# A retention and two-layer mixture kernel on one Trainium2 core: its opening written in the program's own order, with the loads laid out anew

## The chip, the cores and the metric

One NeuronCore of a Trainium2 chip runs the whole program. The metric is device time in microseconds (us), lower is better. The core has five engines with a queue of their own: PE (TensorE, the matrix engine), DVE (VectorE), ACT (ScalarE), POOL (GpSimd) and SP (SyncE, which here only issues DMAs). Each engine takes its instructions strictly in the order in which they stand in its queue.

## What is computed

Attention with a decay instead of a softmax, over 4 batches, 8 heads, 576 positions and 64 channels, feeds a mixture of 4 experts (all used for each token, weighted by given probabilities), which feeds a second mixture of 8 experts of which each token uses one.

```python
scores = scale * np.matmul(q, k.transpose(0, 1, 3, 2))
Dmat = np.where(rel >= 0, gamma[:, None, None] ** rel[None, :, :], 0.0)
x = np.matmul(scores * Dmat[None], v)            # -> 2304 tokens x 512
for e in range(4):                               # first mixture, hidden width 1024
    h = np.maximum(x @ w1[e], 0.0)
    out += p[:, e:e + 1] * (h @ w2[e])
...                                              # second mixture: one of 8 experts per token
```

## The kernel before, in words

Attention goes in 36 steps of 64 positions (`NSTEP`, 9 steps to a batch). Step s has four small groups of float32 matmuls, 8 instructions each (the trace counts 16, two passes to an instruction): the scores (`at_scores`, L258, tile `sc<-qkr`), what the state of the past adds (`at_past`, L278, `uo<-qkr,sn`), scores times values (`at_b`, L290, `uo<-pf,vkr`), and the step's share of the next state (`at_state`, L302, `uo<-vkr,ks`). Between them stand DVE's masking of the scores (`pf`, L268), its four updates of the state (`sn`, L327; `at_sum`) and its scaling of the result (`xf`, L344), POOL's decayed keys (`ks`, L242; `at_split`), and the split of the result into two float16 parts: the high part on ACT (L346), the low part on DVE for the first block, on POOL later (`at_out`, L348 and L350).

Every large product is made of three float16 products of such halves. So the weights are split too: `w_load` brings a float32 piece of 512 KB into one of four buffers `wr`, `w_split` makes the high half on ACT (L191) and the low half on DVE (L192), twice for each piece. Tokens go in 9 blocks of 256 (`NB`), which is four steps to a block. The first expert's first layer (`l1_first`, L533, `ph<-xc,wm`) has four units of 48 matmuls for a block; for block 0 each unit comes in halves of 24 matmuls of 128 columns, so that steps 0 and 1 are enough for the first halves. After a unit, ACT and DVE make the two halves of the hidden values (`keep`, `ht`, L519 and L520). The second layer (`l2`, L685, `po<-wm,ht`) has four units of 12 matmuls of 512 columns for a block. While it runs, `at_hook` adds an attention step after each unit, and `w_do` takes from a list (`w_todo`) the loads and mixings that make sums of the weight quarters for later experts (`mix`, L461 and L462; `x_mix`, `x_keep` and `x_store`, L357, L365, L366 and L369, do the same for x).

What sets the order: in the kernel before, the opening (L1088 to L1157) is written in Python in a certain order, and the tile framework's scheduler then puts the instructions of each engine in an order of its own; where the text says `tc.issue_after`, an instruction may not stand ahead of a given one. SP takes a load only when its buffer is free, and in its queue's order, so a load that waits holds up all behind it. The opening writes a few loads, then runs `opening(s)` for steps 0 to 5, each with the split of step s + 2 and the loads of step s + 4 behind it, with weight splits and half units between them. In `at_step(s)` the scores and the state of step s + 1 go ahead of the result of step s.

Of the kernel before, what the change touches and what calls it, by code (L numbers as in the profile page):

```python
# [126 lines left out]
    return at, np.ascontiguousarray(np.concatenate(cols, axis=1))  # L127


@with_exitstack  # L130
def kernel(
    ctx: ExitStack,
# [88 lines left out]
    def at_load(s):  # L221
        load_qk(s)
        load_vk(s)
# [75 lines left out]
            if uos[s][2] is not None:  # L299
                after(mm, uos[s][2])  # L300

    def at_state(s, on):  # L302

        if s % NC == NC - 1:
            return
        t, ks = raws[s]
        uo = uos[on][0]
        for h in HEADS:
            b2, b1, b0 = _bits(h)
            pe.matmul(  # L310
                uo[rows(b0 ^ b1), b0, C * b2:C * b2 + C], lhsT=ks[rows(b1), 2 * b2 + b0],
                rhs=t[rows(b1), 8 + b2 if b0 else 2 * b2 + b1], start=first(on, b0, b0 ^ b1), stop=True, skip_group_check=True,
            )

    def at_sum(s, on):
        c = s % NC
        if c == NC - 1:
            return
        u = uos[on][0][:, :, 0:2 * C].rearrange("p a (b d) -> p a b d", b=2)
        sn = at_1.tile([128, 2, 2, D], F32, name="sn")  # L320
        if c == 0:
            dve.tensor_copy(out=sn, in_=u)
        else:
            old = st[s - 1]
            for i in range(4):
# [44 lines left out]

    def at_step(s):

        at_open(s)
# [7 lines left out]
        at_out(s)  # L381

    def ago(s, b):
        return s - max(NS * b + NS - 1, NS + 1)
# [39 lines left out]
            sp.dma_start(out=r, in_=w1[e, :, i])  # L424
        rw[e, i] = r

    def w_split(e, i):
        r = rw.pop((e, i))
        if i < KD:
            r = r.rearrange("p (k f) -> p k f", k=KD)  # L430
            for k in range(2):
                t = w1_part(k, i // 2)[:, :, :, 256 * (i % 2):256 * (i % 2) + 256]
                split(r[:, 2 * k:2 * k + 2], t[:, :, 0], t[:, :, 1], S_W)
        else:
            j = 2 * (i - KD)
            for k in range(2):
                split(
                    r[:, 512 * k:512 * k + 512].rearrange("p (h d) -> p h d", h=2), w2_row(j + k, 0), w2_row(j + k, 1), S_W
                )

# [237 lines left out]
    def l2(b, i, h):  # L678
        t = b * TB + i
        if h == 0:  # L680
            pos[b, i] = ps_o[0].tile([128, 2, DM // 2], F32, tag="o", name="po")
        po = pos[b, i]
        for k in range(4 * h, 4 * h + 4):
            for n, (x, y) in enumerate(TERMS):
                pe.matmul(  # L685
                    po,
                    lhsT=hts[k // 2][:, x, k % 2, i * 128:(i + 1) * 128],
                    rhs=w2_row(k, y),
                    start=(k == 0 and n == 0),
                    stop=(k == KF - 1 and n == 2),  # L690
                )
        if h:
            act.activation(out=acc[:, t, 0:DM].rearrange("p (a d) -> p a d", a=2), in_=po, func=ACTF.Copy, scale=p_sb[:, t, 0:1])
# [391 lines left out]
        )  # L1085


    at_load(0)  # L1088
    sp.dma_start(out=ka, in_=ca)
    at_load(1)  # L1090
    w_tiles(0)
    w_load(0, 0, True)
    at_load(2)
    w_load(0, 1, True)
    w_load(0, 2, True)
    at_load(3)
    w_load(0, 3, True)
    dve.memset(acc[:, :, DM:ROW], 0.0)
    pool.memset(acc[:, BM * TB:, 0:DM], 0.0)
# [9 lines left out]
    at_split(0)  # L1109
    at_scores(0)  # L1110
    at_open(-1)
    at_state(0, -1)
    at_sum(0, -1)
    at_split(1)
    opening(0)
    opening(1)
    w_split(0, 0)
    w_load(0, 4)
    l1_first(0, 0, 0, 1)
    w_split(0, 1)  # L1120
    w_load(0, 5)
    l1_first(0, 1, 0, 1)
    opening(2)
    w_split(0, 2)
    w_load(0, 6)
    l1_first(0, 2, 0, 1)
    w_split(0, 3)
    w_load(0, 7)
    sp.dma_start(out=p_sb, in_=probs)
    opening(3)  # L1130
    l1_first(0, 3, 0, 1)
    l1_first(0, 0, 1, 2)
    w_split(0, 4)
    opening(4)
    l1_first(0, 1, 1, 2)
    w_split(0, 5)
    l1_first(0, 2, 1, 2)
    w_split(0, 6)
    opening(5)
    l1_first(0, 3, 1, 2)  # L1140
    w_split(0, 7)
# [4 lines left out]
    sp.dma_start(out=wgr, in_=wg)  # L1146
    sp.dma_start(out=kb, in_=cb)
    sp.dma_start(out=k16, in_=c16)
    ps_sum = at_1.tile([128, NT, 1], F32, name="ps_sum", bufs=1)
    dve.tensor_reduce(out=ps_sum, in_=p_sb, axis=AX.X, op=ALU.add)  # L1150
    dve.tensor_scalar(out=ps_sum, in0=ps_sum, scalar1=1e-9, scalar2=None, op0=ALU.add)
    ps_inv = at_1.tile([128, NT, 1], F32, name="ps_inv", bufs=1)
    dve.reciprocal(out=ps_inv, in_=ps_sum)
    dve.scalar_tensor_tensor(
        out=p_sb, in0=p_sb, scalar=SO1, in1=ps_inv.to_broadcast([128, NT, E1]), op0=ALU.mult, op1=ALU.mult
    )
    split(wgr, wg_sb[:, 0], wg_sb[:, 1], S_G)  # L1157

    nxt = [NS + 2]
    n_stage = 16 * E2  # L1160
# [5 lines left out]
    def at_hook():  # L1166
        s = nxt[0]
        if s >= NSTEP + 4:
            return
        nxt[0] += 1  # L1170
        if s + 4 < NSTEP:
            load_vk(s + 4)
        if s + 3 < NSTEP:
            load_qk(s + 3)
        if s + 2 < NSTEP:
            at_split(s + 2)
        for b in range(NB):
            if ago(s, b) == 1:
                x_mix(b, 0)
        if s < NSTEP:  # L1180
            at_step(s)
        for b in range(NB):
            n = ago(s, b)
            if n == 2:
                x_store(b, 0)
# [280 lines left out]
```

## Time and profile before

| | us |
|---|---|
| runs shown: lowest, median, highest of 3 | 996.5, 999.72, 1002.97 |
| the profiled execution's own time | 998.96 |
| span of its instructions | 997.0 |
| PE busy in the span | 960.9 |

The span is the time from the first to the last instruction of the profiled execution; its own time is 1.96 us longer. In the timeline a row gives the start (us from the span's start), the duration, engine, source line, operation, the tile written and those read, how many instructions are put together, and in brackets how long the engine had been idle before and what released it. "PEclk" is the clock that TensorE was granted as a share of its full 2.4 GHz; 0.5 is 1.2 GHz.

### The profile page before, as it was taken

The page shows a single profiled execution, that of the slowest core. Times are in us where ns is not written, and L with a number is a line of the kernel's source. Part 1 is how long each engine was busy: PE and PEld are TensorE (multiplying, and loading weights), DVE is VectorE, ACT ScalarE, POOL GpSimd, SP SyncE. Part 2 cuts the span into 40 slices and gives each one's busy share as a digit, 9 for nine tenths or more (in the row PEclk, how much of TensorE's full clock was granted, in tenths as well). Part 3 has the DMA queues.
Part 4 walks back from the last instruction along what each step waited for, and adds up shares of the span by engine and source line. Part 5 has one row for each costly group of instructions (what it writes and reads, how often), then busy time and mean ns, then how long its engine had stood idle before and what let it go on. Part 6 is the DMA issues. An engine that isn't in the chain of part 4 may idle for free. (4 is left out here: it accounts for less than half of the span.)

```text
span 997.0 us, 31905 instructions
## 1 busy us (share of the span) xinstructions
PE 960.9 (96%) x13507; PEld 827.5 (83%) x13507; DVE 577.3 (58%) x1296; ACT 534.2 (54%) x1017; POOL 411.7 (41%) x433
## 2 busy tenths in 40 slices
PE   5799999999999999999999999999999999999995
PEld 5576667899999999999999999999987677777773
DVE  5765571475677777766776775888888211211210
ACT  3445453677767777776787686676643122212221
POOL 3577764645555244455442454342323222112111
PEclk9999999999999999999999999999999999999998
DMA  9879774345457778467668726879835616554691
GB/s 335 283 260 328 279 236 166 109 126 181 165 185 217 231 257 270 133 207 211 207 195 309 251 80 174 251 208 232 234 113 199 233 44 229 207 218 146 256 393 48
DMA packets 95939, 209.48 MB, mean 210 GB/s; under 512 B 21486, under 2 KB 42222, under 8 KB 93488
## 3 DMA queue, kind: packets, MB, share of 16 engines
q1 hardware_dynamic: 82784, 159.20, 48.0%
q0 software_dynamic: 13008, 48.20, 15.2%
q8 instruction: 108, 1.77, 0.7%
q14 instruction: 39, 0.32, 0.1%
HBM read 197.88 MB, written 52.99 MB: 252 GB/s over the span
## 5 line engine op out<-in xcount | busy, mean ns | idle before, releaser
L646 PEld LDWEIGHTS <-op 128*128 128x128 f16 x2604 | 245.6, 98 | 26.0 <-POOL s L197 0.7
L580 POOL TENSOR_TENSOR op<-sm,op 128x512 f16<-128x512 f32 x124 | 142.2, 1157 | 223.9 <-ACT op L579 223.8
L561 PEld LDWEIGHTS <-wm_a 128*128 128x128 f16 x3264 | 192.9, 98 | 3.9
L561 PE MATMUL ph<-xc,wm_a 128*128 128x128 f16 x2112 | 132.2, 219 | 0.0
L579 ACT ACTIVATE op<-sm 128x512 f16<-128x512 f32 x124 | 77.6, 634 | 86.7 <-DVE sm L584 86.7
L1068 DVE SCALAR_TENSOR_TENSOR h_s<-p_h,h_s 128x512 f16<-128x512 f32 x40 | 27.6, 691 | 159.1 <-ACT h_s L1067 144.1
L1075 PE MATMUL p_y<-wm_a,h_s 128*128 128x512 f16 x480 | 107.2, 379 | 0.5 <-DVE h_s L1068 0.5
L646 PE MATMUL pv<-wm_a,op 128*128 128x256 f16 x792 | 97.4, 273 | 0.0
L646 PE MATMUL px<-wm_a,op 128*128 128x256 f16 x744 | 91.3, 272 | 0.7 <-DVE acc L654 0.7
L1075 PEld LDWEIGHTS <-h_s 128*128 128x128 f16 x480 | 46.7, 98 | 52.4 <-DVE h_s L1068 0.7
L207 DVE TENSOR_TENSOR s<-pz,s 128x512 f16<-128x512 f32 x111 | 74.0, 683 | 15.6 <-ACT s L206 15.6
L561 PEld LDWEIGHTS <-wm_b 128*128 128x128 f16 x1296 | 76.9, 98 | 1.4
L1078 POOL DMA_INDIRECT out_dram<-y_s,sidxm x17 | 17.2, 1013 | 146.4 <-ACT y_s L1077 128.9
L205 ACT ACTIVATE pz<-sr 128x512 f32<-128x512 f32 x111 | 65.6, 605 | 14.4 <-DVE rk L804 8.8
L464 POOL TENSOR_TENSOR wr<-wr 128x512 f32<-128x512 f32 x48 | 60.4, 1270 | 29.9 <-ACT pz L205 29.2
L1067 ACT ACTIVATE h_s<-p_h 128x512 f16<-128x512 f32 x40 | 23.9, 597 | 78.9 <-PE p_h L1058 74.9
L206 ACT ACTIVATE s<-pz 128x512 f16<-128x512 f32 x111 | 64.0, 599 | 0.6
L1077 ACT ACTIVATE y_s<-p_y,x_g 128x512 f32<-128x512 f32 x20 | 13.7, 687 | 92.8 <-PE p_y L1075 79.2
L654 DVE SCALAR_TENSOR_TENSOR acc<-px,p_sb,acc 128x256 f32<-128x256 f32 x124 | 59.2, 478 | 7.3 <-PE px L646 7.0
L1058 PEld LDWEIGHTS <-wm_b 128*128 128x128 f16 x1056 | 60.0, 98 | 2.8 <-issue 0.6
L1058 PE MATMUL p_h<-x_s,wm_b 128*128 128x128 f16 x1056 | 61.5, 219 | 0.3 <-issue 0.2
L205 ACT ACTIVATE pz<-wr 128x512 f32<-128x512 f32 x100 | 59.4, 609 | 1.5 <-DVE wm_a L207 1.1
(208 smaller groups left out, 1787.3 us busy)
## 6 DMA issues: line engine op xcount, KB each, us to landing
wm_a<-w2d SPq DMA_DIRECT2D x20, 2048.0 KB, 9.6
wr<-in_w_dram SPq DMA_DIRECT2D x40, 512.0 KB, 7.1
wm_b<-w1d SPq DMA_DIRECT2D x10, 2048.0 KB
wm_a<-w1d SPq DMA_DIRECT2D x10, 2048.0 KB
sr<-in_w1s_dram SPq DMA_DIRECT2D x64, 256.0 KB, 3.8
w1d<-s SPq DMA_DIRECT2D x64, 256.0 KB, 4.7
sr<-in_w2s_dram SPq DMA_DIRECT2D x64, 256.0 KB, 5.1
w2d<-s SPq DMA_DIRECT2D x64, 256.0 KB, 4.7
```

Source lines behind the costliest of these rows:

```text
L205: act.activation(out=z, in_=raw, func=ACTF.Copy, scale=scale)
L206: act.activation(out=hi, in_=z, func=ACTF.Copy)
L207: dve.tensor_tensor(out=lo, in0=z, in1=hi, op=ALU.subtract)
L464: pace["pool"] = pool.tensor_tensor(out=quarter(e, n, k, to), in0=quarter(e, n, k, x), in1=quarter(e, n, k, y), op=op)
L561: pe.matmul(bank[:, i], lhsT=w[:, k, u, 128 * i:128 * i + 128], rhs=x[:, v, d, k], start=(first and i == 0 and n == 0), stop=(n == 5), ski ...
L579: act.activation(out=hi, in_=s, func=ACTF.Copy)
L580: pool.tensor_tensor(out=lo, in0=s, in1=hi, op=ALU.subtract)
L646: pe.matmul(out, lhsT=o[a][:, v, k], rhs=w[c][:, k, u], start=(first and n == 0), stop=(n == 11), skip_group_check=True,)
L654: step = dve.scalar_tensor_tensor(out=a, in0=src, scalar=p_sb[:, b * TB + i, e:e + 1], in1=a, op0=ALU.mult, op1=ALU.add)
L1058: pe.matmul(ph[:, j], lhsT=w[k][:, x, f * 128:(f + 1) * 128], rhs=xs[:, y, k], start=(n == 0), stop=(n == 3 * KD - 1),)
L1068: dve.scalar_tensor_tensor(out=lo, in0=ph, scalar=0.0, in1=hi, op0=ALU.max, op1=ALU.subtract)
L1075: pe.matmul(po, lhsT=h[:, a, k], rhs=w[k][:, b], start=(n == 0), stop=(n == 3 * KF - 1))
```

## The change

The opening is rewritten, and each of its instructions is tied to the order in which the program text has it.

- A wrapper `InOrder` around the five engines calls `tc.keep_in_program_order` on every instruction until the opening's end, so the scheduler no longer moves them. In a profile of the changed kernel all of these instructions carry the wrapper's line, L139.
- The loads all stand ahead of the opening, in a new order: the constants `ka` ahead of the first values, the fourth piece of w1 directly behind the second and third, then alternately the pieces of w2 and the steps 4 to 9.
- `at_out` is taken apart into `at_x` (DVE) and `at_parts` (ACT and POOL), and the low half of x is made on POOL for block 0 as well.
- The state of step s stands right ahead of step s (`opened`), no longer in step s - 1. The low half of the second part of two of the four pieces of w2 is made on POOL (`split_p`).
- The seventh step's (s = 6) decayed keys, scores and state, which stood in the opening, now stand in the first unit of layer 2, behind the opening's last POOL instruction; x's mixing and storing on POOL may not stand ahead of the POOL instruction before it; the list of weight mixings begins two units later.

```diff
+class InOrder:
+    def __getattr__(self, name):
+        f = getattr(self.engine, name)
+        def issue(*args, **kw):
+            return self.tc.keep_in_program_order(f(*args, **kw))
+        return issue
...
-    pe, act, dve, pool, sp = nc.tensor, nc.scalar, nc.vector, nc.gpsimd, nc.sync
+    pe, act, dve, pool, sp = [InOrder(tc, e) for e in (nc.tensor, nc.scalar, nc.vector, nc.gpsimd, nc.sync)]
...
         act.activation(out=hi, in_=xf, func=ACTF.Copy)
-        if b:
-            pace["pool"] = pool.tensor_tensor(out=lo, in0=xf, in1=hi, op=ALU.subtract)
-        else:
-            dve.tensor_tensor(out=lo, in0=xf, in1=hi, op=ALU.subtract)
+        pace["pool"] = pool.tensor_tensor(out=lo, in0=xf, in1=hi, op=ALU.subtract)
...
+    for i in range(1, KD):
+        w_load(0, i, True)
+    at_load(3)
+    w_load(0, KD)
+    at_load(NS)
+    w_load(0, KD + 1)
+    at_load(NS + 1)
+    w_load(0, KD + 2)
+    w_load(0, KD + 3)
...
     def opening(s):
-        at_step(s)
-        at_split(s + 2)
-        load_vk(s + 4)
-        if s < NS + 1:
-            load_qk(s + 4)
+        at_open(s)
+        at_past(s)
+        at_b(s)
+        at_x(s)
+
+    def opened(s):
+        at_state(s, s - 1)
+        at_sum(s, s - 1)
+        del uos[s - 1]
...
+    l1_first(0, 0, 1, 2)
+    w_split(0, KD)
+    l1_first(0, 1, 1, 2)
+    later_step(NS)
+    at_split(NS + 1)
+    w_split(0, KD + 1, split_p)
+    l1_first(0, 2, 1, 2)
+    later_step(NS + 1)
+    l1_first(0, 3, 1, 2)
+    w_split(0, KD + 2)
+    w_split(0, KD + 3, split_p)
...
+        if s == NS + 2:
+            with tc.issue_after(pace["pe"].ins), tc.issue_after(pace["pool"].ins):
+                at_split(s)
+                at_split(s + 1)
+                at_split(s + 2)
+                at_open(s)
+                at_scores(s)
+                at_state(s, s, 4 * C)
+                at_sum(s, s, 4 * C)
...
-            if (b, u) == (0, 0):
+            if (b, u) == (0, 2):
                 w_todo.extend([w_loads(0, 0, 2), w_loads(0, 1, 3)] + w1_steps(0) + [lambda: None])
```

The order of PE's first instructions before: the scores of the first three steps stand ahead of the first state.

```order
L263 MATMUL sc<-qkr 64x64 x24
L310 MATMUL uo<-vkr,ks 64x64 x8
L295 MATMUL uo<-pf,vkr 64x64 x8
L310 MATMUL uo<-vkr,ks 64x64 x8
L286 MATMUL uo<-qkr,sn 64x64 x8
L295 MATMUL uo<-pf,vkr 64x64 x8
L310 MATMUL uo<-vkr,ks 64x64 x8
L263 MATMUL sc<-qkr 64x64 x5
```

And now, up to the third step's last group, behind which the first unit of layer 1 stands.

```order
L139 MATMUL sc<-qkr 64x64 x8
L139 MATMUL uo<-vkr,ks 64x64 x8
L139 MATMUL sc<-qkr 64x64 x8
L139 MATMUL uo<-pf,vkr 64x64 x8
L139 MATMUL uo<-vkr,ks 64x64 x8
L139 MATMUL uo<-qkr,sn 64x64 x8
L139 MATMUL uo<-pf,vkr 64x64 x8
L139 MATMUL sc<-qkr 64x64 x8
L139 MATMUL uo<-vkr,ks 64x64 x8
L139 MATMUL uo<-qkr,sn 64x64 x8
L139 MATMUL uo<-pf,vkr 64x64 x8
```

The groups of steps 0 and 1 moved ahead of the third step's scores; the fourth step's scores, which stood here, moved behind three half units.

SP's queue before, from the first piece of w1 to the first two pieces of w2 (`qkr` and `vkr` are a step's queries with keys, and its values with keys; `wr` with 4x256 is a piece of w1, with 1024 one of w2).

```order
L422 DMA wr<-in_w_dram 128x4x256
L228 DMA qkr<-in_qk_dram 128x640
L234 DMA vkr<-in_vk_dram 128x640
L422 DMA wr<-in_w_dram 128x4x256 x2
L228 DMA qkr<-in_qk_dram 128x640
L234 DMA vkr<-in_vk_dram 128x640
L422 DMA wr<-in_w_dram 128x4x256
L234 DMA vkr<-in_vk_dram 128x640
L228 DMA qkr<-in_qk_dram 128x640
L234 DMA vkr<-in_vk_dram 128x640
L228 DMA qkr<-in_qk_dram 128x640
L420 DMA wr<-in_w_dram 128x1024 x2
```

And the same stretch now.

```order
L139 DMA wr<-in_w_dram 128x4x256
L139 DMA qkr<-in_qk_dram 128x640
L139 DMA vkr<-in_vk_dram 128x640
L139 DMA wr<-in_w_dram 128x4x256 x3
L139 DMA qkr<-in_qk_dram 128x640
L139 DMA vkr<-in_vk_dram 128x640
L1196 DMA wgr<-in_wg_dram 128x64
L1197 DMA kb<-in_cb_dram 128x330
L1198 DMA k_84<-in_c_dram 128x256
L139 DMA wr<-in_w_dram 128x1024
L139 DMA qkr<-in_qk_dram 128x640
L139 DMA vkr<-in_vk_dram 128x640
```

The fourth piece of w1 moved ahead of the fourth step's two loads, three small tables that were loaded much later moved into the opening, and the pieces of w2 stand one by one between the steps.

POOL's queue now, from the keys of step 5 (`ks_570`) to those of steps 6, 7, 9 and 10 (`ks_720`, `ks_722`, `ks_811`, `ks_851`; step 8 needs none). `wm` are low halves of w2, `xc_565` the low half of block 1's x, `xf_207` block 0's x, whose sums are made in place.

```order
L139 TENSOR_TENSOR ks_570<-vkr_139,ka_101 128x256
L139 TENSOR_TENSOR wm_c_82<-wr_135,wm_c_82 128x2x256
L139 TENSOR_TENSOR xc_565<-xf_566,xc_565 128x4x64
L139 TENSOR_TENSOR wm_a_78<-wr_143,wm_a_78 128x2x256
L256 TENSOR_TENSOR ks_720<-vkr_147,ka_101 128x256
L256 TENSOR_TENSOR ks_722<-vkr_152,ka_101 128x256
L373 TENSOR_TENSOR xf_207<-xf_207 128x256
L256 TENSOR_TENSOR ks_811<-vkr_158,ka_101 128x256
L373 TENSOR_TENSOR xf_207<-xf_207 128x256
L256 TENSOR_TENSOR ks_851<-vkr_716,ka_101 128x256
L373 TENSOR_TENSOR xf_207<-xf_207 128x256 x2
L382 TENSOR_TENSOR xc_206<-xf_207,xc_206 128x512 x2
```

Before, it had there (`ks_452` and `ks_563` are steps 5 and 6, `ks_675`, `ks_813` and `ks_853` steps 7, 9 and 10, `xf_189` block 0's x).

```order
L242 TENSOR_TENSOR ks_452<-vkr_245,ka_101 128x256
L242 TENSOR_TENSOR ks_563<-vkr_363,ka_101 128x256
L357 TENSOR_TENSOR xf_189<-xf_189 128x256 x2
L369 DMA xcd_89<-xc_188 256x1x1024
L357 TENSOR_TENSOR xf_189<-xf_189 128x256 x2
L242 TENSOR_TENSOR ks_675<-vkr_454,ka_101 128x256
L348 TENSOR_TENSOR xc_558<-xf_559,xc_558 128x4x64
L242 TENSOR_TENSOR ks_813<-vkr_677,ka_101 128x256
L348 TENSOR_TENSOR xc_558<-xf_559,xc_558 128x4x64
L366 TENSOR_TENSOR xc_188<-xf_189,xc_188 128x512
```

The keys of step 6, which stood directly behind those of step 5, moved behind two low halves of w2, and block 0's sums moved from ahead of step 7's keys to behind them.

## Rows read from the trace of the kernel before

**Rows 1.** The page's busy times: PE, of the whole span.

```profile
PE 960.9 (96%) x13507; PEld 827.5 (83%) x13507; DVE 577.3 (58%) x1296; ACT 534.2 (54%) x1017; POOL 411.7 (41%) x433
```

**Rows 2.** Stretches: length, busy PE, PEld, DVE, ACT, POOL, clock, DMA share, GB/s.

```profile
15.00:20.00 5.00, 4.52 (x103) 3.90 (x96) 4.34 (x15) 1.96 (x4) 1.58 (x2) 0.67 1.06 409
...
30.00:35.00 5.00, 3.00 (x44) 2.88 (x42) 5.00 (x11) 1.87 (x4) 2.42 (x4) 0.88 0.87 322
35.00:40.00 5.00, 4.99 (x98) 3.83 (x96) 3.96 (x15) 1.83 (x6) 2.53 (x4) 0.78 0.54 151
```

**Rows 3.** Waits of PE in its first 60 us: total, times, longest.

```profile
PE sc L263 <- DMA qkr<-in_qk_dram: 10.2, 4, 3.4
...
PE sc L263 <- DVE pf L268: 1.3, 1, 1.3
```

**Rows 4.** The timeline of PE, at seven places.

```profile
11.30 0.68 PE L295 MATMUL uo<-pf,vkr 64*64 64x64 f32 x16
...
16.99 0.40 PE L533 MATMUL ph<-xc,wm_a 128*128 128x128 f16 x2
...
29.64 1.51 PE L533 MATMUL ph<-xc,wm_a 128*128 128x128 f16 x24
...
38.72 2.76 PE L685 MATMUL po<-wm_c,ht 128*128 128x512 f16 x12
...
57.73 1.16 PE L533 MATMUL ph<-xc,wm_a 128*128 128x256 f16 x9
...
66.33 0.83 PE L533 MATMUL ph<-xc,wm_c 128*128 128x256 f16 x6
...
69.57 0.41 PE L295 MATMUL uo<-pf,vkr 64*64 64x64 f32 x16
```

**Rows 5.** The timeline of POOL and ACT where a landing released them.

```profile
8.22 0.61 POOL L242 TENSOR_TENSOR ks<-vkr,ka 128x256 f32<-128x256 f32 x1 [0.97 <-DMA vkr<-in_vk_dram]
11.19 0.76 POOL L242 TENSOR_TENSOR ks<-vkr,ka 128x256 f32<-128x256 f32 x1 [2.36 <-DMA vkr<-in_vk_dram]
...
9.52 1.15 ACT L191 ACTIVATE wm_a<-wr 128x512 f16<-128x512 f32 x2 [7.48 <-DMA wr<-in_w_dram]
12.49 1.15 ACT L191 ACTIVATE wm_a<-wr 128x512 f16<-128x512 f32 x2 [1.82 <-DMA wr<-in_w_dram]
13.82 0.63 ACT L191 ACTIVATE wm_c<-wr 128x512 f16<-128x512 f32 x1 [0.19 <-DMA wr<-in_w_dram]
...
18.05 0.63 ACT L191 ACTIVATE wm_c<-wr 128x512 f16<-128x512 f32 x1 [1.22 <-DMA wr<-in_w_dram]
```

**Rows 6.** The timeline of DVE, ACT and POOL: what one operation takes alone.

```profile
17.23 0.42 DVE L268 TENSOR_TENSOR pf<-sc,ka 128x256 f32<-128x256 f32 x1
17.56 0.85 DVE L327 SCALAR_TENSOR_TENSOR sn<-sn,ka,uo 128x64 f32<-128x64 f32 x4
...
18.66 0.68 DVE L192 SCALAR_TENSOR_TENSOR wm_c<-wr,wm_c 128x512 f16<-128x512 f32 x1
...
20.36 0.38 ACT L519 ACTIVATE ht<-ph 128x256 f16<-128x256 f32 x1 [1.17 <-PE ph L533]
...
39.19 0.67 POOL L348 TENSOR_TENSOR xc<-xf,xc 128x256 f16<-128x256 f32 x1 [2.36 <-ACT xc L346]
39.98 1.15 POOL L366 TENSOR_TENSOR xc<-xf,xc 128x512 f16<-128x512 f32 x1
...
49.27 0.72 POOL L357 TENSOR_TENSOR xf<-xf 128x256 f32<-128x256 f32 x1
```

**Rows 7.** The timeline of DVE and POOL where both work on SBUF at once.

```profile
28.19 2.44 DVE L192 SCALAR_TENSOR_TENSOR wm_c<-wr,wm_c 128x512 f16<-128x512 f32 x2
...
34.73 1.53 POOL L348 TENSOR_TENSOR xc<-xf,xc 128x256 f16<-128x256 f32 x1 [2.51 <-ACT xc L346]
```

**Rows 8.** Waits of PE from 60 to 160 us: first and last of six.

```profile
PE uo L286 <- DVE xf L344: 1.2, 2, 0.9
...
PE po L685 <- issue: 0.2, 1, 0.2
```

More of the change, by code (lines that the diff above doesn't have):

```diff
@@ L310, in at_state, with at_sum @@
             pe.matmul(
-                uo[rows(b0 ^ b1), b0, C * b2:C * b2 + C], lhsT=ks[rows(b1), 2 * b2 + b0],
+                uo[rows(b0 ^ b1), b0, at + C * b2:at + C * b2 + C], lhsT=ks[rows(b1), 2 * b2 + b0],
                 rhs=t[rows(b1), 8 + b2 if b0 else 2 * b2 + b1], start=first(on, b0, b0 ^ b1), stop=True, skip_group_check=True,
             )
-    def at_sum(s, on):
+    def at_sum(s, on, at=0):
         c = s % NC
@@ L371, in at_step @@
     def at_step(s):
-        at_open(s)
+        if s not in uos:
+            at_open(s)
         at_past(s)
@@ L425, in w_load, with w_split @@
         rw[e, i] = r
-    def w_split(e, i):
+    def w_split(e, i, f=split):
         r = rw.pop((e, i))
@@ L436, in w_split @@
             for k in range(2):
-                split(
+                (f if k else split)(
                     r[:, 512 * k:512 * k + 512].rearrange("p (h d) -> p h d", h=2), w2_row(j + k, 0), w2_row(j + k, 1), S_W
@@ L684, in l2 @@
             for n, (x, y) in enumerate(TERMS):
-                pe.matmul(
+                pace["pe"] = pe.matmul(
                     po,
@@ L1085, in m_l2 @@
         )
-    at_load(0)
+    dve.memset(acc[:, :, DM:ROW], 0.0)
+    pool.memset(acc[:, BM * TB:, 0:DM], 0.0)
+    load_qk(0)
     sp.dma_start(out=ka, in_=ca)
+    load_vk(0)
     at_load(1)
@@ L1093, with later_step @@
     at_load(2)
-    w_load(0, 1, True)
-    w_load(0, 2, True)
+    for i in range(1, KD):
+        w_load(0, i, True)
     at_load(3)
-    w_load(0, 3, True)
-    dve.memset(acc[:, :, DM:ROW], 0.0)
-    pool.memset(acc[:, BM * TB:, 0:DM], 0.0)
-    def opening(s):
-        at_step(s)
-        at_split(s + 2)
-        load_vk(s + 4)
-        if s < NS + 1:
-            load_qk(s + 4)
+    w_load(0, KD)
[4 more added lines that the diff above has]
+    w_load(0, KD + 3)
+    at_load(NS + 2)
+    sp.dma_start(out=p_sb, in_=probs)
+    at_load(NS + 3)
+    at_load(NS + 4)
+    load_vk(NS + 5)
+    def opening(s):
+        at_open(s)
+        at_past(s)
+        at_b(s)
+        at_x(s)
+    def opened(s):
+        at_state(s, s - 1)
+        at_sum(s, s - 1)
+        del uos[s - 1]
     at_split(0)
+    at_split(1)
+    at_open(-1)
     at_scores(0)
[L1111 to L1114, printed above, removed]
+    opened(0)
+    at_scores(1)
     opening(0)
+    at_parts(0)
+    opened(1)
     opening(1)
     w_split(0, 0)
-    w_load(0, 4)
+    at_split(2)
+    at_parts(1)
+    at_scores(2)
+    opened(2)
+    opening(2)
+    w_split(0, 1)
+    at_parts(2)
     l1_first(0, 0, 0, 1)
-    w_split(0, 1)
-    w_load(0, 5)
+    w_split(0, 2)
     l1_first(0, 1, 0, 1)
-    opening(2)
-    w_split(0, 2)
-    w_load(0, 6)
+    w_split(0, 3)
     l1_first(0, 2, 0, 1)
-    w_split(0, 3)
-    w_load(0, 7)
-    sp.dma_start(out=p_sb, in_=probs)
+    at_split(3)
+    at_scores(3)
+    l1_first(0, 3, 0, 1)
+    opened(3)
     opening(3)
-    l1_first(0, 3, 0, 1)
+    at_parts(3)
+    at_split(4)
+    def later_step(s):
+        at_scores(s)
+        opened(s)
+        opening(s)
+        at_parts(s)
     l1_first(0, 0, 1, 2)
-    w_split(0, 4)
-    opening(4)
+    w_split(0, KD)
     l1_first(0, 1, 1, 2)
-    w_split(0, 5)
+    later_step(NS)
+    at_split(NS + 1)
+    w_split(0, KD + 1, split_p)
     l1_first(0, 2, 1, 2)
-    w_split(0, 6)
-    opening(5)
+    later_step(NS + 1)
     l1_first(0, 3, 1, 2)
-    w_split(0, 7)
+    w_split(0, KD + 2)
+    w_split(0, KD + 3, split_p)
+    del uos[NS + 1]
+    pe, act, dve, pool, sp = nc.tensor, nc.scalar, nc.vector, nc.gpsimd, nc.sync
     open_ctx.close()
@@ L1148 @@
     sp.dma_start(out=k16, in_=c16)
[L1149 to L1157, printed above, removed]
+    with tc.issue_after(pace["act"].ins), tc.issue_after(pace["dve"].ins):
+        ps_sum = at_1.tile([128, NT, 1], F32, name="ps_sum", bufs=1)
+        dve.tensor_reduce(out=ps_sum, in_=p_sb, axis=AX.X, op=ALU.add)
+        dve.tensor_scalar(out=ps_sum, in0=ps_sum, scalar1=1e-9, scalar2=None, op0=ALU.add)
+        ps_inv = at_1.tile([128, NT, 1], F32, name="ps_inv", bufs=1)
+        dve.reciprocal(out=ps_inv, in_=ps_sum)
+        dve.scalar_tensor_tensor(
+            out=p_sb, in0=p_sb, scalar=SO1, in1=ps_inv.to_broadcast([128, NT, E1]), op0=ALU.mult, op1=ALU.mult
+        )
+        split(wgr, wg_sb[:, 0], wg_sb[:, 1], S_G)
     nxt = [NS + 2]
@@ L1174, in at_hook @@
             load_qk(s + 3)
-        if s + 2 < NSTEP:
+        if NS + 2 < s < NSTEP - 2:
             at_split(s + 2)
+        if s == NS + 2:
[3 more added lines that the diff above has]
+                at_split(s + 2)
+                at_open(s)
+                at_scores(s)
+                at_state(s, s, 4 * C)
+                at_sum(s, s, 4 * C)
         for b in range(NB):
             if ago(s, b) == 1:
-                x_mix(b, 0)
+                with tc.issue_after(pace["pool"].ins):
+                    x_mix(b, 0)
         if s < NSTEP:
@@ L1184, in at_hook @@
             if n == 2:
-                x_store(b, 0)
+                with tc.issue_after(pace["pool"].ins):
+                    x_store(b, 0)
                 x_mix(b, 1)
```

23 lines of the change are left out of this document (15 added, 8 removed).

## The prediction

> **What bounds the kernel now.** I read the busy times first, then the waits of PE, then the stretches of the opening, then the timeline. PE is busy for 960.9 of 997.0 us [rows 1], so all that a new order can win is the 36.1 us in which PE stands, and the stretches in which it works at half clock. Of the waits, 10.2 us are the first scores waiting for loads, all in the first 15 us [rows 3]; a bound of 3.3 us is the first landing itself. The stretches show the rest: from 30 to 35 us PE works 3.00 of 5 us, and around 17 to 20 and 34 to 37 us its clock falls to half (mean 0.67 and 0.88, then 0.78) [rows 2]. Beyond 60 us only 4.2 us of waits follow in the next 100 us (six kinds, 1.2 us the largest) [rows 8]. The change touches the first 60 us, and the order of all engines is the same again long before the middle of the program. So I follow one quantity: when does PE reach certain places? Before, layer 1's first unit starts at 16.99, layer 2's first unit at 38.72, block 1's first unit at 57.73 and its third at 66.33 us [rows 4]. What these places gain is what the time gains, less what comes back later.
>
> **The landings.** Up to the third piece of w1 the same bytes stand ahead, so I keep the landings: second step's values 8.22, first piece 9.52, third step's values 11.19, second piece 12.49, third 13.82 us [rows 5]. A piece of 512 KB takes 13.82 - 12.49 = 1.33 us, so the fourth, now directly behind, lands at 15.1 instead of shortly before 18.05 [rows 5]. The fourth step's two loads (320 KB each, 0.83 us each at this rate) fall behind it, to 16.8 us. DMA is full in this stretch either way (share 1.06 [rows 2]); the order of landings changes, not their sum.
>
> **Part 1: the order up to layer 1.** PE's groups of float32 matmuls last 0.68 us at first and 0.41 us later [rows 4]. The first matmuls thus run as at half clock; I take 0.5 us a group up to 13.5 us and 0.25 us from there, with the same ratio. The second step's keys are made by 8.22 + 0.61 = 8.9, the third's by 11.19 + 0.61 = 11.8 [rows 5]. The states and results of steps 0 and 1 no longer wait behind the third scores and are done by 10.6. Then state 2 at 11.9. Its masked scores stand on DVE behind the first piece's two low halves: ACT's two high halves take 1.15 us [rows 5] behind the first x (9.9 to 11.0), the two low halves 0.6 us apart (12.3), masking 0.42 (12.6), the last group 12.9 to 13.4. Layer 1 starts at 13.4 instead of 16.99: 3.6 us early. The low half of step 1's x is off DVE; on POOL it takes 0.67 [rows 6] behind the third keys and ends by 12.4, so it is hidden.
>
> **Part 2: eight half units.** Units of 24 matmuls take about 1.4 us at full clock [rows 4] and 2.7 at half. The first starts within the half-clock stretch, so I give it 2.7, and its result is there at 16.3. From here ACT is in the way: its queue has the high halves of piece three behind the first unit's `ht` (0.38 us [rows 6]), so piece three is split at 16.7 + 1.2 + 0.7 = 18.6, and unit three starts there. Piece four follows by 20.1; unit four runs 20.3 to 21.8. Step 3's state update now stands on DVE behind the fourth `ht`: 22.7 + 0.8 [rows 6] + 0.3 for `xf` = 23.8; the high half on ACT ends at 24.3, the low one on POOL at 25.0. So PE stands from 22.3 to 25.1. Two half units follow, to 28.0. Step 4's masking waits on DVE for the fifth piece's low halves and another `ht`, so the group after it runs at 29.7; the seventh half unit takes 29.9 to 31.5. Step 5's masking stands behind that unit's `ht`, which on ACT stands behind three conversions of the sixth piece (1.7 us): 34.1. The eighth half unit runs 34.4 to 35.8 and layer 2 starts at 35.8 instead of 38.72. Of 3.6 us won, 2.9 are left.
>
> **Part 3: layer 2 of block 0.** Twelve matmuls take 2.7 us [rows 4], step 6's scores 0.25, three more matmuls 0.7: PE is at 39.4. Then comes state 6, which was part of the opening before. Its keys stand on POOL behind the second low half of w2's last piece. On ACT that needs the last `ht` (36.4) and six conversions of about 0.54: 39.3. POOL takes 1.15 for a low half of 512 columns and 0.61 for the keys [rows 5, 6]: 41.2. PE stands for 1.8 us. From there 33 matmuls (7.4 us) and some 20 groups (5.0 us) lead to block 1, with 0.3 us of waits: 54.0 instead of 57.73. The wait of 1.3 us for the masking, held up by a weight mixing [rows 3], goes because the mixings begin two units later; they are not saved but done later, on DVE, where 4.2 us of waits over 100 us already stand [rows 8]. I let those be as they were.
>
> **Part 4: POOL's backlog.** From 40.5 us POOL has block 0's four sums (0.72 each), two low halves of 1.15, the low halves of steps 6 and on (0.67) and each step's keys (0.61) [rows 5, 6], in a row without a gap, where before the sums were done while PE still worked on layer 1. Adding them up: keys of step 11 at 50.1, of 12 at 53.1, of 13 at 59.1. PE wants these at 53.3, 55.5 and 58.3. So 0.8 us are lost at step 13, and block 1's third unit starts at 63.1 instead of 66.33: 3.2 us early.
>
> **Part 5: the clock.** Before, the clock fell to half twice, behind stretches in which PE had long waits; the means stand for 5 x (1 - 0.67) x 2 = 3.3 us and 5 x (0.12 + 0.22) x 2 = 3.4 us at 1.2 instead of 2.4 GHz [rows 2]. In the new order PE stands 2.8 us up to 25.1, some 2 us up to 34.2 and 1.8 us up to 41.2, so it falls again somewhere; no row tells where. A stretch of 3.4 us at half clock costs at most half of it, 1.7 us, where PE is the last, and nothing where it waits for ACT or DVE anyway. Both ends with the whole sum: no further stretch, 3.2 us won; three stretches at the worst places, 5 us lost and 1.8 slower than before. I take one stretch, nearly on the path: 1.4 us.
>
> **The sum.** 3.2 - 1.4 = 1.8 us. Against the profiled execution's own 998.96 that is 997.2; against the median of the runs shown, 999.72, it is 997.9. I forecast 997.5 us. This is 0.2%, well within the 1% that a measurement can tell here.
>
> **What POOL costs DVE.** The price that I put at nothing is the contention of POOL and DVE. Alone, a low half of 512 columns takes DVE 0.68 [rows 6]; next to POOL's sums two take 2.44, and POOL's own low half of x takes 1.53 next to DVE's instead of 0.67 [rows 6, 7]. The change moves six low halves from DVE to POOL (four of 256 columns, two of 512), where they meet DVE's low halves of w1. By the rows one such meeting costs up to 0.9 us; I find two (around 12 and 15 us), of which PE sees 0 to 0.9 each, and take nothing, since both end before PE asks. The Trainium skill ("GPSIMD Engine Reference", Key points) says that POOL shares its SBUF interfaces with VectorE, with contention when a DVE instruction has two SBUF inputs, and that elementwise work is about twice as fast on DVE. The rows agree with the first (0.68 against 1.22 each); alone, POOL's 0.67 for 256 columns and 1.15 for 512 against DVE's 0.42 and 0.68 are 1.6 to 1.7 times. By that rule the moved work costs 6 low halves' difference, about 2 us of POOL, which are in the sum already.
>
> **Rivals.**
> First, POOL becomes the bound and the kernel gets slower. Place: layer 2 of block 0, keys of steps 11 to 13. From 40.5 to 62 us POOL is full in my sum, so each stretched instruction shows at step 13. If a quarter of its 21 us of work is stretched as in [rows 7] (up to double), 5 us come in; it decides once more than 3 us are added, since that is what is won before. Price: 998.96 - 3.2 + 1.4 + 5 = 1002.2. For it: [rows 7]. Against: DVE's operations there read one operand from PSUM, and in [rows 6] at 39 to 50 us POOL works at its short times.
> Second, PE falls to half clock two or three times, and the gain is gone: 998.96 - 3.2 + 3 to 5 = 998.8 to 1000.8. For it: waits of 2 us in every stretch from 22 to 41. Against: between its waits PE works without a gap here, and part of the cost falls into time in which it waits anyway.
> Third, the order won is worth more than my chain: PE stays at full clock, and the 4.2 us of later waits mostly go too, since DVE has less to do in the opening: 998.96 - 3.2 - 3.5 = 992.3. For it: the low halves off DVE (4 x 0.4 + 2 x 0.6 = 2.8 us of its busiest stretch). Against: the mixings put off come back on DVE there.
> Fourth, the change doesn't do what it says: the loads limit it and the new order only waits elsewhere. That would be 999. The first units speak against it: the third piece lands at 13.8, 4.8 us before its unit starts in my chain, so ACT and DVE are in the way, not DMA.
>
> **Chances.** My forecast (a gain of 0.5 to 4 us) 0.42; clock falls and the gain is gone, 0.18; more than my chain, 0.22; POOL the bound and slower, 0.13; no effect 0.05. The bounds of the clock and of POOL's stretching reach up to 1002, those of the third rival down to 991: the range is 991 to 1002. Cases of both signs hold the chance; the forecast's own range is 995 to 998.5. Faster by over 1% needs below 989.7, which only a still larger third rival gives: 0.06. Slower by over 1% needs above 1009.7: 0.02. Within 1%: 0.92.
>
> **What would show it.** Right: the first matmul of layer 1 (the first `ph`) at 13 to 14 us; the first `po` near 36 to 37; a wait of PE for POOL's `ks` of 1 to 2 us behind the first `po` unit; POOL without a gap from 40 to 60 us; block 1's first unit (`ph` of 256 columns) at 54 to 56. Wrong: a first `po` below 33 or above 39, ACT's conversions of the sixth piece not in front of an `ht`, no wait for step 6's keys, or a difference in the total that does not already stand at 66 us.

## The result, and the profile after

The changed kernel takes 1011.77 us (median of 4 runs, 1009.16 to 1014.21) against 999.85 us for the kernel before (4 runs): a ratio of 1.0119, 95% interval 1.0076 to 1.0163. It is slower by 12 us, where 997.5 had been forecast. Its profiled execution took 1009.16 us (span 1007.4).

Busy times on the page of the changed kernel, for [rows 1]:

```profile
PE 964.0 (96%) x13507; PEld 828.9 (82%) x13507; DVE 574.7 (57%) x1290; ACT 535.0 (53%) x1019; POOL 416.2 (41%) x439
```

PE has the same instructions; it stands for 43.4 us of the span instead of 36.1, and is 3.1 us longer at its work. To see where, first the places of [rows 4] in the timeline of PE after:

```profile
13.43 3.97 PE L139 MATMUL ph<-xc,wm_a 128*128 128x128 f16 x48
...
24.18 0.22 PE L139 MATMUL ph<-xc,wm_a 128*128 128x128 f16 x1 [1.62 <-ACT xc L139]
24.93 4.19 PE L139 MATMUL ph<-xc,wm_a 128*128 128x128 f16 x47 [0.53 <-POOL xc L139]
...
33.70 0.46 PE L139 MATMUL uo<-vkr,ks 64*64 64x64 f32 x16 [1.01 <-POOL ks L139]
...
36.44 2.75 PE L704 MATMUL po<-wm_c,ht 128*128 128x512 f16 x12
...
41.47 0.33 PE L277 MATMUL sc<-qkr 64*64 64x64 f32 x2 [1.13 <-DVE pf L282]
41.62 0.45 PE L324 MATMUL uo<-vkr,ks 64*64 64x64 f32 x16
...
47.66 0.46 PE L277 MATMUL sc<-qkr 64*64 64x64 f32 x16 [1.42 <-DVE xf L358]
...
57.20 1.16 PE L552 MATMUL ph<-xc,wm_a 128*128 128x256 f16 x9
...
66.19 0.40 PE L300 MATMUL uo<-qkr,sn 64*64 64x64 f32 x11 [0.85 <-issue]
...
67.28 0.83 PE L552 MATMUL ph<-xc,wm_c 128*128 128x256 f16 x6
```

The two largest of its waits up to 60 us, for [rows 3]:

```profile
PE uo L139 <- POOL ks L139: 5.0, 4, 2.2
PE sc L139 <- DMA qkr<-in_qk_dram: 3.5, 1, 3.5
```

The opening is faster: the first matmul of layer 1 at 13.43 instead of 16.99, the first of layer 2 at 36.44 instead of 38.72. The loss comes later. Five stretches of the changed kernel (columns as in [rows 2]):

```profile
20.00:40.00 20.00, 16.30 (x343) 13.16 (x336) 11.64 (x36) 8.79 (x20) 4.92 (x7) 0.91 0.81 291
...
60.00:80.00 20.00, 19.15 (x408) 14.56 (x407) 15.05 (x42) 11.69 (x23) 15.37 (x23) 1.00 0.76 255
80.00:100.00 20.00, 15.26 (x270) 9.32 (x272) 6.81 (x20) 6.55 (x13) 11.55 (x18) 0.83 0.63 218
120.00:140.00 20.00, 18.40 (x382) 13.45 (x377) 10.04 (x29) 8.12 (x18) 16.01 (x23) 1.00 0.82 280
140.00:160.00 20.00, 15.38 (x316) 9.60 (x307) 12.60 (x34) 12.02 (x25) 12.74 (x16) 1.00 0.62 183
```

And two of them in the kernel before:

```profile
80.00:100.00 20.00, 20.00 (x401) 13.93 (x399) 10.33 (x30) 8.84 (x18) 13.33 (x19) 1.00 0.98 333
...
140.00:160.00 20.00, 19.69 (x307) 12.66 (x306) 8.38 (x24) 8.52 (x18) 13.93 (x20) 1.00 0.75 255
```

From 80 to 100 us PE works 15.26 instead of 20.00 us, partly at half clock (0.83), and from 140 to 160 15.38 instead of 19.69. Who keeps it? The waits of ACT from 60 to 180 us (total, times, longest), after:

```profile
ACT xm L381 <- DMA xcd<-xm: 18.1, 3, 7.7
...
ACT xo L365 <- DMA xcd<-xo: 3.7, 1, 3.7
```

The kernel before has one such wait in its attention:

```profile
ACT xm L365 <- DMA xcd<-xm: 6.5, 1, 6.5
```

`xm` holds the second half of x of a block from block 2 on. It has one buffer. ACT writes its high part (`x_keep`, L381), POOL the low part, and POOL stores it to `xcd`; the next block's conversion must wait until that store has landed. What hangs on the wait is read by following one case over four engines. The changed kernel, POOL, ACT, DVE and PE, each in order of time:

```profile
78.00 0.68 POOL L385 DMA_DIRECT2D xcd<-xm  x1 [0.30 <-POOL xm L382]
...
79.27 3.20 POOL L373 TENSOR_TENSOR xf<-xf 128x256 f32<-128x256 f32 x4
...
85.03 0.63 ACT L381 ACTIVATE xm<-xf 128x512 f16<-128x512 f32 x1 [5.32 <-DMA xcd<-xm]
...
86.91 0.57 ACT L220 ACTIVATE wm_a<-pz 128x512 f16<-128x512 f32 x1
...
88.01 0.60 ACT L220 ACTIVATE wm_a<-pz 128x512 f16<-128x512 f32 x1
...
87.51 0.69 DVE L221 TENSOR_TENSOR wm_a<-pz,wm_a 128x512 f16<-128x512 f32 x1 [6.31 <-ACT wm_a L220]
88.64 0.69 DVE L221 TENSOR_TENSOR wm_a<-pz,wm_a 128x512 f16<-128x512 f32 x1 [0.43 <-ACT wm_a L220]
89.24 0.41 DVE L282 TENSOR_TENSOR pf<-sc,ka 128x256 f32<-128x256 f32 x1
...
82.26 2.76 PE L704 MATMUL po<-wm_a,ht 128*128 128x512 f16 x12
89.71 0.71 PE L277 MATMUL sc<-qkr 64*64 64x64 f32 x16 [4.69 <-DVE pf L282]
...
91.53 4.12 PE L704 MATMUL po<-wm_a,ht 128*128 128x512 f16 x12
```

The store issued at 78.00 is waited for until 85.03. Behind the conversion stand the high halves of two weight pieces in ACT's queue (86.91, 88.01), behind these their low halves in DVE's (87.51, 88.64), and behind these the masking that PE waits for: 4.69 us without work. Then PE runs at the lower clock: the groups take 0.71 instead of 0.46 us, the unit of layer 2 4.12 instead of 2.76. In the kernel before, the same place:

```profile
76.72 0.68 POOL L369 DMA_DIRECT2D xcd<-xm  x1 [0.30 <-POOL xm L366]
...
82.60 1.15 ACT L365 ACTIVATE xm<-xf 128x512 f16<-128x512 f32 x2 [1.59 <-POOL xf L357]
83.66 0.58 ACT L206 ACTIVATE wm_a<-pz 128x512 f16<-128x512 f32 x1
...
84.27 0.69 DVE L207 TENSOR_TENSOR wm_a<-pz,wm_a 128x512 f16<-128x512 f32 x1 [3.35 <-ACT wm_a L206]
84.87 0.41 DVE L268 TENSOR_TENSOR pf<-sc,ka 128x256 f32<-128x256 f32 x1
...
86.14 0.46 PE L263 MATMUL sc<-qkr 64*64 64x64 f32 x16
87.00 2.76 PE L685 MATMUL po<-wm_a,ht 128*128 128x512 f16 x12
```

There ACT waits for POOL's sums, not for the store; only one weight piece stands behind, since the others are already split; the masking starts at 84.87 and PE does not wait. The sums are ready at nearly the same time in both kernels (82.60 there; the row at 79.27 of the changed kernel ends at 82.47). It is the store that comes later in the changed kernel: it is issued at 78.00 instead of 76.72, and is waited for until 7.0 us after its issue, where it took at most 5.9 us before. So this fourth unit of block 1's layer 2, which starts at 87.00 before, starts at 91.53 after: 4.5 us late, where the third (83.45 before, 82.26 after) was 1.2 us early. The second case is like the first:

```profile
153.81 0.63 ACT L381 ACTIVATE xm<-xf 128x512 f16<-128x512 f32 x1 [5.09 <-DMA xcd<-xm]
...
156.00 0.69 DVE L221 TENSOR_TENSOR wm_a<-pz,wm_a 128x512 f16<-128x512 f32 x1 [3.97 <-ACT wm_a L220]
...
160.25 0.42 DVE L358 TENSOR_TENSOR xf<-uo,ka 128x256 f32<-128x256 f32 x1
...
160.81 0.46 PE L300 MATMUL uo<-qkr,sn 64*64 64x64 f32 x16 [3.56 <-DVE xf L358]
```

The table follows the start of one unit, the last of layer 2, from block to block (read from PE's timelines):

| fourth unit of | before | changed | difference |
|---|---|---|---|
| block 1 | 87.00 | 91.53 | +4.5 |
| block 2 | 119.12 | 124.19 | +5.1 |
| block 3 | 150.77 | 161.67 | +10.9 |
| block 4 | 180.61 | 191.51 | +10.9 |

The loss comes in two steps, at blocks 1 and 3, and ACT's longest wait for the store lies in neither:

```profile
123.77 1.15 ACT L381 ACTIVATE xm<-xf 128x512 f16<-128x512 f32 x2 [7.71 <-DMA xcd<-xm]
124.83 0.71 ACT L365 ACTIVATE xo<-xf 128x256 f16<-128x256 f32 x2
125.44 0.67 ACT L712 ACTIVATE acc<-po,p_sb 128x512 f32<-128x512 f32 x1
```

Behind this conversion stands no weight piece, and the unit of block 2 starts at 124.19 with only 0.6 us more of a loss than the one of block 1. The length of a wait does not tell its cost; these cases differ in what stands behind it.

### The profile page after: what moved, and what is told of

Its sections match the earlier page's. It is cut to its first block, busy times and chain, and to the rows that moved or that the text cites. A ratio compares the mean times of both kernels' runs of the same rounds, so it can differ in the third digit from the quotient of the medians.

```text
span 1007.4 us, 31908 instructions
## 1 busy us (share of the span) xinstructions
PE 964.0 (96%) x13507; PEld 828.9 (82%) x13507; DVE 574.7 (57%) x1290; ACT 535.0 (53%) x1019; POOL 416.2 (41%) x439
## 5 line engine op out<-in xcount | busy, mean ns | idle before, releaser
L219 ACT ACTIVATE pz<-sr 128x512 f32<-128x512 f32 x111 | 65.6, 605 | 15.6 <-DVE rk L823 9.1
L221 DVE TENSOR_TENSOR wm_a<-pz,wm_a 128x512 f16<-128x512 f32 x62 | 42.0, 689 | 39.4 <-ACT wm_a L220 38.9
```

What stands on the lines that cost most here:

```text
L219: act.activation(out=z, in_=raw, func=ACTF.Copy, scale=scale)
L221: dve.tensor_tensor(out=lo, in0=z, in1=hi, op=ALU.subtract)
```

## The experiments

Three parts of the change reach beyond the opening: the two ties (`issue_after` around x's sums and around the store of the first half of x, for all blocks), the weight mixings begun two units later, and what the opening leaves behind. Theory A: the conversions of `xm` come too early against a store out of a single buffer, because of the ties. Theory B: the late mixings. Theory C: the opening itself. A ratio is that of the times to the kernel before in the same comparison; its 95% interval stands in brackets. 0.001 is 1 us.

**Undoing parts of the change.** Ties off from block 2 on:

```diff
-                with tc.issue_after(pace["pool"].ins):
-                    x_mix(b, 0)
+                if b < 2:
+                    with tc.issue_after(pace["pool"].ins):
+                        x_mix(b, 0)
+                else:
+                    x_mix(b, 0)
...
```

and the same around `x_store(b, 0)`.

> The changed kernel, but from block 2 on x's sums and the store of the first half of x are free again to stand ahead of the POOL instruction before them, as in the kernel before; the opening and the late mixings stay. Theory A (ACT's conversions of xm come to the head of ACT's queue while POOL's store of the block before is still under way, because the four sums now stand in a row): ACT's waits for that store fall from 18.1 us to under 8, layer 2's matmul 96 is reached near 88 instead of 94.3 us, and the time is 997 to 1001 us, ratio to before 0.998 to 1.001. Theory B (the mixings put off by two units are what stands in the way): the three losses of 6.6, 3.4 and 3.6 us stay, 1009 to 1012. Theory C (the new opening itself): also 1009 to 1012.

Measured: 1003.15 us, 1.0040 [1.0013, 1.0067]. 8 of the 12 us come back; ACT's waits for the store fall only to 12.4 us, the unit above starts at 88.41.

Mixings early again (`(b, u) == (0, 0)` in `w_plan`):

> The changed kernel with the list of weight mixings begun at layer 2's first unit again, as before; ties and opening stay. Theory A: the waits of ACT for the store of xm stay at 15 us or more and the time at 1007 to 1012. Theory B: all three losses go, 996 to 1000, and layer 2's matmul 96 is reached below 89 us; some 1.3 us come back around 41 us, where the masking stands behind a mixing. Theory C: 1009 to 1012.

Measured: 1014.71 us, 1.0135 [1.0099, 1.0171]. Theory B alone falls: with the ties in place early mixings help nothing. Theory A has the time, but not the 15 us of waits: the wait for the store shrinks to 7.9 us, and 6.4 us of waiting for POOL's sums take the place of the rest. PE waits 3.2 us in layer 2's first units.

Both undone, for every block:

> The changed kernel with both undone: sums and stores free for every block, mixings from layer 2's first unit; what is left is the new opening and the seventh step in layer 2's first unit. Theories A and B: no losses beyond 80 us, 996 to 1000. Theory C: 1009 to 1012, with losses of 3 us or more after 80 us in this run too.

Measured: 999.78 us, 0.9992 [0.9972, 1.0011]. Theory C falls: opening and seventh step neither cost nor bring anything that can be measured. ACT still waits 10.2 us for the store in this run, without a loss.

One tie each, from block 2 on. First the store tied, the sums free:

> The changed kernel, where from block 2 on only the sums are free and the store of the first half of x keeps its tie. If the sums in a row are what costs: as with both ties off, 1002 to 1005. If the store's place is what costs (two stores close behind each other): 1008 to 1012.

Measured: 1012.56 us, 1.0147 [1.0121, 1.0172], waits for the store of `xm` 20.5 us. My expectation that the sums in a row are what costs was wrong. The counterpart:

> The changed kernel, where from block 2 on only the store of the first half of x is free and the sums keep their tie: the counterpart of the run with the store tied and the sums free (1012.56 us). Store theory: as with both ties off, 1001 to 1005, ACT's waits for the store of xm below 14 us. Sums theory: 1008 or more.

Measured: 1006.30 us, 1.0057 [1.0031, 1.0083], 16.1 us of waits: between the two theories. Against 1.0040 with neither, the sums' tie alone costs 2 us, the store's alone 11, both together 8. Why the place of the first half's store lengthens the waits for the second's is not settled.

**The buffer.** A ring of three for both halves:

```diff
-name="xo", bufs=2)
+tag="xo", name="xo", bufs=3)
...
-name="xm", bufs=1)
+tag="xo", name="xm", bufs=3)
```

> The changed kernel, where the second half of x in block 2 and later (xm, one buffer) and the first half (xo, two buffers) share one ring of three buffers of the same size, so that a conversion of xm waits for the store of two halves ago and not of the last. Theory A: ACT's wait for the store of xm goes to under 3 us, with it the losses at 84 to 94 and 156 to 163 us, and the time is 997 to 1002, though the ties stay. Theories B and C: the buffer does not matter, 1008 to 1012.

Measured: 1003.34 us, 1.0023 [1.0008, 1.0039]: the time that theory A wanted, but 8.9 us of waits for the store were left, so this run didn't show the reason. A cleaner way gives `xm` a second place of its own, in rows of `acc` that are not written yet:

```diff
+            if b % 2:
+                xos[b][1] = acc[:, (BM - 1) * TB:BM * TB, 0:DM].bitcast(F16).rearrange("p a (c k t) -> p a c k t", c=4, k=2)
+            else:
+                xos[b][1] = at_1.tile([128, 2, 4, 2, HB], F16, name="xm", bufs=1)
```

> The changed kernel, ties and late mixings as they are, but the second half of x (xm) of every odd block lies in the rows of acc that stay unwritten until block 4's second layer: xm so has two places of its own, and a conversion waits for the store of two blocks ago. The ring of three did not show this, since a wait for a store of 3.6 and 4.9 us stayed in it. Theory A (ACT stands for the store out of the one buffer): no wait of ACT xm for xcd from 60 to 180 us, layer 2's matmul 96 below 91 us instead of 94.3, time 997 to 1002 although the ties stay. Theory D (the ties cost by POOL's order, the four sums ahead of keys and low halves, whatever the buffer): the waits go over to POOL's sums or keys, 1004 or more.

Measured: 1002.94 us, 1.0034 [1.0018, 1.0050], and no wait of ACT `xm` for `xcd` at all. Nothing else was edited, so some 8.5 of the 12 us hang on the one buffer. What is left at the place above, ACT and PE of this run:

```profile
82.20 0.63 ACT L384 ACTIVATE acc<-xf 128x512 f16<-128x512 f32 x1 [3.03 <-POOL xf L373]
...
86.88 0.70 PE L277 MATMUL sc<-qkr 64*64 64x64 f32 x16 [2.40 <-DVE pf L282]
...
88.70 3.44 PE L707 MATMUL po<-wm_a,ht 128*128 128x512 f16 x12
```

The conversion now waits for the four sums that the tie puts in a row (theory D in part), and PE still 2.40 us. Ties off and two places together:

> The kernel without the ties from block 2 on and, besides, two places for xm. Theory A: the 12.4 us of ACT's waits for the store that were left without the ties go, with them the wait of PE of 2.7 us at 87 us; layer 2's matmul 96 at 88 us and the time 996 to 1000, ahead of 1003.15. Theory D: with the ties off the buffer no longer matters, 1002 to 1004.

Measured: 1000.74 us, 1.0000 [0.9978, 1.0022]. The unit above starts at 87.60; the loss is gone.

**One part at a time in the kernel before.** The ties alone:

> The kernel before with nothing changed but the two ties (x's sums and the store of the first half not ahead of the POOL instruction before them). Theory A: the ties alone bring the waits for the store, 10 us or more of ACT's time, and the kernel is slower, 1003 to 1009. A rival (the ties harm only together with the new opening or the late mixings): 998 to 1001.

Measured: 1008.85 us, 1.0098 [1.0073, 1.0124]. The rival falls, but theory A's 10 us of waits for the store are not there either: they are 7.1 us, and 6.4 us more are for POOL's sums. The late mixings alone:

> The kernel before with nothing changed but the list of weight mixings, begun two units later. Theory A: harmless by itself, or a loss of up to 3 us where a split stands behind a conversion of xm: 998 to 1003. Theory B (the late list is a loss of its own): 1004 or more.

Measured: 1006.37 us, 1.0076 [1.0047, 1.0106]: theory B again, and more than I expected. ACT's waits there, 60 to 180 us:

```profile
ACT xm L365 <- DMA xcd<-xm: 14.6, 3, 7.6
```

In the two runs block 1's third unit of layer 2 starts 3.3 and 3.6 us earlier than before (80.19, 79.87), the fourth of block 4 6.5 and 7.8 later (187.09, 188.43). Each edit wins in the first 80 us and loses more behind. With two places for `xm`, the late mixings:

> The kernel before with the mixings begun two units later and two places for xm; with one place it was 1006.37 us. If the late mixings cost through the store of xm (14.6 us of ACT's waits there): 998 to 1001. If splits and mixings in the wrong place cost by themselves: 1004 or more.

Measured: 998.98 us, 0.9988 [0.9973, 1.0003], so their whole loss went through the store. The two losses (9.8 and 7.6 us alone) do not add up: the changed kernel, which has both, loses 11.9. The ties:

> The kernel before with the two ties on all blocks and two places for xm; with one place it was 1008.85 us. If the ties cost through the store of xm (7.1 us in one wait there): 999 to 1003. If by POOL's order (6.4 us of ACT's waits were for the sums): 1004 or more.

Measured: 1002.83 us, 1.0027 [1.0008, 1.0046]: 7 of 10 us through the store. The rest fits POOL's order (ACT waits 10.0 us for the sums there, 6.8 in the control that follows), but no run shows that this is its reason. As a control two places alone:

> The kernel before with two places for xm and nothing else. If the second place only repairs what ties or late mixings bring: 998 to 1000.5, as before. If it is a gain of its own (one wait of 6.5 us of ACT): 994 to 997, and what it gives back elsewhere would be that much smaller as a repair.

Measured: 1001.17 us beside 1001.96, 0.9990 [0.9976, 1.0004]. The second place is a repair, and by the interval at most 2.4 us of a gain.

**Keeping a gain.** Ties on blocks 0 and 1 alone, the rest as before:

> The kernel before with the two ties for blocks 0 and 1 alone. Of the ties on all blocks the run before showed both: 3.7 us won up to layer 2's matmul 48 (52.2 instead of 55.9 us) and 10.3 us lost behind it. On every engine the order behind block 1 is now that of the kernel before. Theory A (the loss comes from the ties from block 2 on): the 3.7 us stay won to the end, 995 to 998, ratio 0.995 to 0.998. Theory E (behind the opening the engines stand against something that does not begin earlier, stores or loads, so whatever is won in the first 60 us is lost by 160): 999 to 1001.

Measured: 998.55 us, 0.9997 [0.9983, 1.0012]: theory E by its time. But the profile has 1.6 us still won at block 2's fourth unit (117.49 instead of 119.12), and lost at block 3's (152.31), where ACT waits 9.0 us for the store. With two places:

> The same with two places for xm. Theory A: the one wait for the store that is left there (6.5 us of ACT in the kernel before) goes too, the time is 0 to 2 us below the run without: 994 to 997. Theory E: 999 to 1001 if loads are what it stands against, 996 to 998 if it is the stores of xm.

Measured: 997.53 us, 0.9977 [0.9959, 0.9994]; in its profile the gain stays to the end (block 4's fourth unit 179.13 instead of 180.61). The time lies 0.5 us outside theory A's range and inside what theory E has for the stores of `xm`. Both put what was lost down to the store; that is not proof, since the two intervals overlap and the trace puts PE's own wait of 2.8 us in the run before down to issue. A last version begins the mixings one unit later as well:

> The kernel before with ties on blocks 0 and 1, two places for xm, mixings one unit later. If the wait of 2.4 us for the scaling and the masking around 45 us is due to the mixing: that wait goes, 994.5 to 997. If the later mixings push splits behind the conversions of xm again: 998 to 1001.

Measured: 998.32 us beside 1001.96, 0.9968 [0.9954, 0.9981]: faster than the kernel before by 3 us. This is the lowest ratio of all runs, though its interval overlaps with that of the run before. The wait it was aimed at did not go: PE waits 2.4 us for the scaling at 44.93, as in the run before, and block 4's fourth unit starts at 179.06, against 179.13. So the later mixings are not shown to bring anything. The changed kernel's own opening with the same help:

> The changed kernel's opening and seventh step, with the ties for blocks 0 and 1 alone, the mixings from layer 2's first unit, and two places for xm. Theory A: nothing is left that costs behind 80 us, but the early mixings cost 2 to 3 us around 45 to 52 us as in the run with early mixings and all ties: 998 to 1001. If what is left is the opening's gain, 996 to 998.

Measured: 1001.84 us, 1.0019 [1.0004, 1.0034], with a wait of 3.2 us for the scaling in layer 2's first units. With the mixings one unit later:

> The changed kernel's opening, ties on blocks 0 and 1 alone, two places for xm, mixings begun one unit later than before instead of two (or none, 1001.84 us). If the mixing that stands ahead of the masking around 45 to 52 us is what takes the opening's gain (a wait of 3.2 us there): that wait goes to under 1.5 us, 996 to 999. If the opening's gain is lost anyway: 1000 to 1003.

Measured: 1001.41 us, 1.0015 [0.9990, 1.0041]. That wait is gone, the time is no better; what takes the opening's gain there stays open.

## Why the prediction was wrong

- **The opening (parts 1 and 2) was right.** Layer 1 at 13.4 was forecast, 13.43 came; a halt up to 25.1, it ended at 24.93; layer 2 at 35.8, it was 36.44. One wait had another reason: at 33.70 PE waited for POOL's keys, where I had named the masking.
- **Part 3 had the time of step 6's state right** (41.2 forecast, 41.62 measured), in part by luck: the wait was for the masking (1.13 us, behind 1.19 us of DVE's work on the probabilities), not 1.8 us for POOL's keys, and that was a sign named beforehand as wrong. Behind it part 3 was too early: block 1 at 54.0, measured 57.20. The 15.6 us in between instead of 12.8 hold a wait of 1.42 us for the scaling at 47.66 where 0.3 of waits were taken, 20 groups that take 6.2 us from start to start instead of 5.0, and 33 matmuls with 7.9 instead of 7.4. The 3.2 us of the sum were read off block 1's third unit (63.1 forecast); it started at 67.28, 0.95 us later than before. By the start of block 1's layer 2 (74.92 instead of 76.35) 1.4 us stood won.
- **The step that failed** is the premise that the change "touches the first 60 us", and with it the end of part 3, where the later waits of PE were left at 4.2 us ("I let those be as they were"): what the change costs behind 60 us was put at nothing. The runs showed 10.9 us of loss by block 3's last unit of layer 2 in its place. The ties alone cost 9.8 us and the late mixings alone 7.6; with two places for `xm` 2.7 and nothing are left of that, and 3.4 of the changed kernel's 11.9. The late mixings leave more weight splits behind the conversions of `xm` (two pieces instead of one at 83 to 88 us). PE's later waits, 1.2 us the largest, were no measure of what could come.
- **Part 4 counted POOL's operations and not its stores.** The operations came nearly as added up: POOL was busy for 19.2 us from 40 to 60 us, and the keys of steps 11, 12 and 13 ended at 50.9, 54.3 and 60.1 instead of 50.1, 53.1 and 59.1. But the ties hold for all blocks, not for block 0's sums only, and `xm` is not free until its store has landed; neither was priced. The trace of before had the row for it, ACT's 6.5 us for `xcd<-xm`; [rows 3] and [rows 8] list PE's waits only.
- **The first rival had the sign, not the mechanism.** POOL's keys for steps 11 to 13 never kept PE: among its waits from 42 to 160 us none is for `ks`.
- **Part 5 held in the opening** (one stretch: 0.91 from 20 to 40 us stands for 3.6 us at half clock, 3.4 were taken) and missed the second, 0.83 from 80 to 100 us, behind the wait of 4.69.
- **What POOL costs DVE** I had put at nothing for PE; layer 1's start at 13.43 agrees. Behind it one low half took DVE 1.10 us at 17.64, beside POOL's keys, and PE waited 0.51 us for it.
- The sign named beforehand for a wrong sum, a difference that does not already stand at 66 us, is what came.

The Trainium skill ("DMA: Bandwidth & Descriptors", Anatomy of one DMA — SWDGE (gpsimd) path) gives a transfer issued by GpSimd some 2 us plus its bytes at 436 GB/s; for 512 KB an estimate by these figures is 3.2 us. The changed kernel's trace has twice that, and the measurement decides (the list of issues in its profile: count, KB each, median us to landing):

```profile
xcd<-xo POOLq DMA_DIRECT2D x7, 512.0 KB, 6.0
xcd<-xm POOLq DMA_DIRECT2D x7, 512.0 KB, 6.8
```

## What to carry to other kernels

A tile with one buffer that is stored from is a clock of its own: before anything ahead of it is moved earlier, or its store later, compare the time from the issue of the store to the next write with the time that the store takes to land, and look at what stands behind that write on its engine: a wait of 7.7 us with nothing of weight behind it cost next to nothing here, one of 5.3 us with two weight pieces behind it 4.7 us of PE. Read the waits of every engine, not of the bounding one alone: a wait of 6.5 us on ACT that costs nothing today can be what the next edit runs into. And an ordering rule that is meant for the opening should be written for the opening's blocks alone.

## What the runs showed of the hardware

A store of 512 KB from POOL's queue took 7.0 us from its issue at 78.00 to the release at 85.03; DMA was busy for 0.76 and 0.63 of the two stretches of 20 us around it. Whether that traffic is the reason no run here tells.

A halt of PE can cost more than it lasts. After the 4.69 us the three groups up to the unit at 91.53 took 1.82 us, against 0.86 in the kernel before (86.14 to 87.00), and the unit 4.12 instead of 2.76: 2.3 us more, half of the halt again. It need not be so: after the wait of 3.56 us at 160.81 the groups took 0.44 to 0.46 us and the granted clock from 160 to 165 us was 1.00, while in the run with two places for `xm` a wait of 2.40 us at 86.88 was followed by groups of 0.70 us and a unit of 3.44. The length of the wait alone does not tell which.
